# Attention and GELU MLP on one normalised input: one summed channel tile ahead of the logits in three of four chunks, q's weights in five loads, and a new order of pieces

## The chip, the cores and the metric

One core of a Trainium2 chip runs the kernel. The metric is the device time of one execution in microseconds (us). The engines work side by side, each through its own list of instructions in order: TensorE (PE, matmuls; PEld is its weight load), VectorE (DVE), ScalarE (ACT), GpSimd (POOL) and SyncE (SP, which here only issues DMAs).

## The reference

The input is normalised once; attention over a dilated window and an MLP both read it, and both are added to the input.

```python
def _A_ref(x, wqkv, wo):                      # x: (1, 2048, 640)
    H = 32; Dh = D // H                       # Dh = 20
    W, dil = 8, 2
    q, k, v = ...                             # x @ wqkv, each (B, H, S, Dh)
    idx = pos[:, None] - off[None, :]         # off = 0, 2, .. 14
    mask = idx >= 0
    kg, vg = ...                              # k and v at idx
    logits = jnp.einsum("bhsd,bhswd->bhsw", q, kg) * scale
    logits = jnp.where(mask[None, None, :, :], logits, -1e9)
    attn = _softmax(logits, axis=-1)
    o = jnp.einsum("bhsw,bhswd->bhsd", attn, vg)
    return (...)(o) @ wo
def _B_ref(x, w1, b1, w2, b2):                # 640 -> 1536 -> 640
    return _gelu(x @ w1 + b1) @ w2 + b2
xn = _layernorm(x, axis=-1)
return x + _A_ref(xn, A_wqkv, A_wo) + _B_ref(xn, B_w1, B_b1, B_w2, B_b2)
```

## The kernel before

The 2048 positions are worked in four chunks of 512, each of four blocks `j` of 128. Channels lie on partitions in five tiles of 128, permuted so that each partition belongs to one of 32 heads: the sum over a head's 20 channels is the sum over five tiles and then over four partitions.

Every step is a small function, recorded as a named piece, and `ORDER` (L40 to L72) lists the pieces by hand. Each engine gets its instructions in that order; between engines only semaphores hold. The names, with n the chunk: `st`, `su`, `sq`, `rs`, `rc`, `xn` are the normalisation (block statistics on DVE, L209, or on ACT, L221 and L228, for block 1 of chunk 0 and for chunks 2 and 3; square root on ACT, reciprocal on DVE). `tp` and `tc` transpose the result to `xnT`, for chunk 0 on PE with copies by DVE and ACT (L280, L285), later by DMA on SP (L292). `wa`, `wb` are matmuls on constants at the start.

- q, k, v: chunk 0 in blocks and pairs of blocks (`ga`, `gb`, `gd`, `ge`, copies `gc`, L349; `hj`, copies `hc`, L380); later chunks by `pj` and the copies `pc` on ACT (L336, L400). Their PSUM banks come from a pool of four, `psA`, shared with the MLP's `f1` (L586), which ACT empties with the GELU `ge` (L602).
- logits: `qk{n}{j}{h}` on DVE multiplies q with k shifted to four of the eight window places (128x2560, into `half`, L433). `pa{n}{j}{k}` on DVE adds channel tiles in place (L465): k = 0 adds tiles 2 and 3 to 0 and 1, k = 1 adds tile 1 to 0, and k = 2, which no chunk uses before, adds tile 4 to 0. How many tiles are left is `KEPT`. `lg` sums what is left over the four partitions of each head with the matrix `head_of`: for each tile kept, two halves h and four blocks j, eight matmuls of 128x512, block j writing 32 of the rows of `L` (L474). `cl` copies `L` out on ACT.
- softmax: `m`, `mx`, `ex` (ACT), `ss`, `ri`, `at`. Then `xd{n}{j}` on SP broadcasts block j's weights to all partitions by DMA (L548), into `ax` or, for odd chunks, into spent room of `x_sb`.
- values: `av{n}{j}{h}` on DVE (L557, again into `half`), `aa` adds the two halves (an accumulating DMA on POOL, L567, for chunks 0 to 2, DVE in chunk 3), `ab` and `ot` on DVE (L573, L577) make `oT`.
- output: `o{n}{bl}{pc}` on PE: pc 0 to 3 are the MLP's second product, pc 4 is `oT` times wo (L622 for 512 columns, L624 for 128). `oc` copies out on ACT, and `od` adds it to the output by an accumulating DMA on POOL (L635); the input and b2 get there by `xp` (SP) and `xb` (POOL).

`half` has one buffer for all chunks: a chunk's `av` may write a block only when the chunk's `lg` has read it, and the next chunk's `qk` only when `ot` has read it.

At the start SP issues block 0 of x, then q's weights as one load, k's, blocks 2 and 3, v's, chunk 1 of x and w1; ACT issues block 1 and b1.

Of the kernel before, what the change touches and what calls it, by code (L numbers as in the profile page):

```python
# [20 lines left out]
KT, FT = D // P, F // P  # L21
# [16 lines left out]
COLS = ((0, 2), (2, 4), (4, 5))  # L38

ORDER = """  # L40
wa ho st00a sum1 st00 rs00 rc00 neg1 sq1 xn00a tp00a wb xn00b tp00b mean1 tc00a rs01 rc01 tb b1 tc00b ga gb2 xn01 tp01
tc01a tc01b gb3 gb4 gd ge gc4 gc1 hj100 st02a st02 rs02 hc100 st03a st03 hj101 gc0 rc02 xn02 rs03 hj102 rc03 xn03
hc101 hc102 tp02 tc02 hj202 tp03 tc03 hj201 hc201 hj010 st11a hc010 st13a hc202 st12a hj012 hc012 hj112 hc112 f10_3
st11 ldx hj011 f10_9 st10a st10 st12 st13 rs1 qk011 ge0_3 rc1 xn13 pad01 qk000 qk001 tc13 ge0_9 xn12 tc12 pa000 qk010
pk hj110 hc110 hj111 hc111 hc011 qk030 qk031 qk021 pad11 xn11 f10_10 tc11 pa010 xn10 qk020 tc10 ge0_10 f10_2 ge0_2
hj200 hc200 f10_0 pa030 f10_6 f10_11 su20 ge0_6 xp2 su22 su23 pj111 pc111 ge0_0 su21 ng2 pj110 pc110 pj104 pc104 sq23
pj120 pc120 ge0_11 sq20 pj114 pc114 pj113 pc113 pa001 pa020 pa021 pj102 pc102 pa031 pa011 lg0 cl0 mask m0 hj212 hc212
pj123 pc123 mx0 ex0 pj103 pc103 pj112 pc112 ss0 ri0 pj101 pc101 pj100 pc100 qk110 qk100 ld2 ldo xb2 sq22 qk130 pj124
pc124 hj211 sq21 qk121 rs2 pj121 pc121 hj210 hc210 rc2 f10_8 qk131 hc211 f11_9 ge1_9 xp0 xn20 f10_1 ge0_1 f10_7 tc20
f11_5 xb0 qk120 xn21 tc21 qk101 ge1_5 ge0_7 xn23 tc23 ge0_8 xn22 qk111 o000 f11_8 ge1_8 pa130 at0 pa110 f11_0 ge1_0  # L50
pa100 pad12 f10_5 ge0_5 f11_3 ge1_3 f11_6 su32 tc22 pa120 pa101 xd00 f10_4 su33 pj214 pc214 pa111 su31 su30 pj210
pc210 pad21 xd02 ge0_4 pj211 pa121 ge1_6 pa131 lg1 pj200 pad02 av000 av001 aa00 pc200 ng3 sq32 sq31 sq30 av020 pc211
av021 xd01 av011 o001 pj213 pc213 pj122 pj202 pc202 av010 o002 ab00 ot00 pj204 pj212 o003 pc212 pj223 pj222 cl1 aa02
xd03 pc122 av030 av031 m1 mx1 sq33 rs3 pj201 rc3 pc204 o004 oc00 ab02 ot02 pj224 ex1 o020 aa01 aa03 ss1 ri1 xn33 at1
ab01 ot01 ab03 o021 o022 o023 o024 xp1 tc33 pc201 xn32 tc32 pc222 oc02 ot03 od02 f12_7 xd10 av101 pad22 xd12 pc223
f11_4 xn30 o030 o031 o032 o033 pc224 xd11 xn31 pj221 av100 aa10 o034 oc03 f11_2 o010 ge1_4 tc31 av120 o011 o012 o013
o014 av110 av111 aa11 ge2_7 pc221 od03 f11_7 ge1_7 pj203 pc203 ge1_2 xd13 f11_1 av131 tc30 pj311 pc311 av130 aa13
pj304 f12_3 ge2_3 pj310 pc310 pc304 ge1_1 pj302 av121 aa12 ab10 ot10 f11_10 pc302 ge1_10 pj313 pc313 qk201 qk200 pj312
pj314 ab11 ot11 qk210 pc312 oc01 od01 f13_8 ge3_8 qk211 o130 ab13 pa200 pc314 f11_11 ge1_11 qk231 f12_6 o131 ot13
qk230 xb3 f12_0 ge2_0 pj220 pc220 o132 o133 o134 oc13 pj301 pc301 pa210 ge2_6 ab12 ot12 qk221 pj300 pj324 pc300 qk220  # L60
f13_7 xb1 pc324 od13 pa211 pj303 o120 pa230 pa220 pa231 pc303 pad31 pa221 pa201 lg2 ge3_7 cl2 qk301 f12_2 m2 mx2 ex2
f13_10 f12_8 ge2_8 o121 o122 o123 od00 o124 oc12 qk310 ss2 pj320 pc320 qk311 ri2 at2 xd22 xd20 o110 o111 qk331 o112
o113 o114 oc11 od11 qk330 f13_6 ge3_6 f12_5 ge2_5 ge3_10 o100 ge2_2 qk320 pa330 qk321 pa320 f13_5 f12_4 ge3_5 pj322
f13_2 o101 ge2_4 qk300 xd21 pc322 pa321 o102 o103 o104 ge3_2 pa300 pa301 pa331 pa310 pa311 lg3 f13_3 av210 f13_9 oc10
od10 od12 av211 aa21 ge3_3 f12_10 ge2_10 xd23 av230 av200 f12_1 ge2_1 ge3_9 av231 aa23 f12_9 ge2_9 f13_1 ge3_1 f13_4
f12_11 av201 av221 ab21 ge3_4 av220 pj321 o210 o211 o212 f13_0 ot21 ge2_11 o213 o214 f13_11 cl3 m3 mx3 ex3 pad32 ss3
ri3 at3 xd32 oc21 o200 o201 pc321 o202 aa20 ab20 ot20 ab23 ot23 ge3_0 aa22 o203 o310 o204 oc20 pj323 pc323 ab22 ot22
av320 o230 o231 o232 o233 o234 od20 oc23 av321 aa32 xd30 o311 o312 od21 ab32 o220 o221 o222 o223 o224 ge3_11 xd31
av311 od23 o313 av301 av310 oc22 od22 o320 o321 o322 o323 av300 ot32 o324 oc32 aa31 ab31 ot31 o314 oc31 o300 o301 o302
xd33 od32 aa30 o330 o303 ab30 ot30 o304 av331 av330 aa33 ab33 o331 o332 o333 ot33 od31 xl o334 oclo oc30 ohi ochi ochd  # L70
od30
""".split()  # L72


# [1 line left out]
def kernel(  # L76
# [55 lines left out]
    def load_w(s):  # L132
        nc.sync.dma_start(wqkv[s][:], wqkv_v[:, :, s * D : (s + 1) * D])
# [43 lines left out]
    mask = consts.tile([H, W, MW], BF16, name="mask")  # L177
# [610 lines left out]
```

## Time and profile before

| | |
|---|---|
| median of three runs | 207.1 us (206.86 to 207.37) |
| the profiled execution | 207.49 us, span of its trace 205.7 us |
| PE busy | 200.8 us, 1285 matmuls |
| DVE busy | 175.4 us |
| ACT busy | 127.7 us |
| first 128x512 product of chunk 0's DVE logits (L433) | starts at 17.40 us |
| q's weights (800 KB, one DMA) | 5.5 us from issue to landing |

A group's row in the profile reads: line, engine, operation, out<-in, shapes, count, then total busy us and mean ns of one, then the engine's idle time just before these instructions and what ended it. A row of waits reads: who waited, for whom, us in total, times, longest. A row of the chain reads: start, length, what.

### The profile page before, as it was taken

What the parts mean: (1) busy time and instruction counts of PE and PEld (TensorE: products, weight loads), DVE (VectorE), ACT (ScalarE), POOL (GpSimd) and SP (SyncE); (2) the same over time, 40 slices, a digit from 0 to 9 for tenths busy, and PEclk for the clock granted to TensorE, in tenths of its full rate; (3) what the DMA queues carried; (4) which work ended last, traced back from release to release, by engine and by line L of the source; (5) the groups of instructions that cost most, each with busy time, mean ns of one, the idle gap of its engine ahead of it and who ended that gap; (6) DMA issues with size and microseconds to landing.
All of it is one profiled execution on the core that took longest, in us unless ns stands there. A gap on an engine that the chain in (4) does not pass through costs nothing.

```text
span 205.7 us, 3262 instructions
## 1 busy us (share of the span) xinstructions
PE 200.8 (98%) x1285; PEld 112.2 (55%) x1285; DVE 175.4 (85%) x214; ACT 127.7 (62%) x242; POOL 34.4 (17%) x49
## 2 busy tenths in 40 slices
PE   7899999999999999999999999999999999999994
PEld 2797745565445555555555554555444555555552
DVE  3489999379998989949999994999979979799981
ACT  5488999899999879916466344834616854221210
POOL 2000000050000422102703303001023420311210
DMA  6999389969258599899996965018209998931244
GB/s 210 390 397 370 75 232 326 403 102 185 64 116 264 99 186 181 142 192 124 207 198 113 144 107 64 0 16 182 41 0 132 162 193 162 192 41 17 30 52 64
DMA packets 27335, 31.77 MB, mean 154 GB/s; under 512 B 9272, under 2 KB 22072, under 8 KB 27320
## 3 DMA queue, kind: packets, MB, share of 16 engines
q0 software_dynamic: 7408, 12.78, 39.4%
q1 hardware_dynamic: 19600, 18.58, 31.4%
q8 instruction: 10, 0.16, 0.3%
q10 hardware_dynamic: 312, 0.20, 0.3%
q14 instruction: 5, 0.04, 0.1%
HBM read 10.00 MB, written 7.54 MB: 85 GB/s over the span
## 4 chain that ended last, share of the span: by engine, by line
PE 95%; DMA 3%; SPq 0%; DVE 0%; issue 0%
PE lo L622 29%; PE hps L586 25%; PE pps L336 24%; PE hi L624 7%; PE gps L380 7%; DMA wq_sb<-in_A_wqkv_dram 3%; PE L L474 2%; PE gps L349 1%; PE tp L280 0%; SPq L130 0%; DVE osb L652 0%
## 5 line engine op out<-in xcount | busy, mean ns | idle before, releaser
L586 PE MATMUL hps<-xnT,w_sb 128*128 128x512 bf16 x240 | 55.6, 379 | 0.0
L433 DVE TENSOR_TENSOR half<-qT,kT 128x2560 bf16<-128x2560 bf16 x32 | 46.2, 1482 | 2.9 <-PE L L474 2.8
L622 PE MATMUL lo<-w_sb,hT 128*128 128x512 bf16 x144 | 41.3, 379 | 0.0
L586 PEld LDWEIGHTS <-w_sb 128*128 128x128 bf16 x240 | 22.9, 98 | 26.3 <-issue 0.8
L629 ACT CAST osb<-lo 128x512 bf16<-128x512 f32 x15 | 8.8, 587 | 36.8 <-PE hi L624 18.5
L624 PE MATMUL hi<-w_sb,hT 128*128 128x128 bf16 x144 | 31.5, 219 | 0.0
L602 ACT ACTIVATE hT<-hps,b1T 128x512 bf16<-128x512 f32 x36 | 24.0, 683 | 10.7 <-PE hps L586 10.7
L465 DVE TENSOR_TENSOR half<-half 128x2048 bf16<-128x2048 bf16 (+1 forms) x32 | 29.0, 952 | 0.2
L635 POOL DMA_DIRECT2D out_dram<-osb x15 | 13.6, 973 | 77.1 <-ACT osb L630 68.5
L557 DVE TENSOR_TENSOR half<-vT,x_sb 128x2560 bf16<-128x2560 bf16 x16 | 22.8, 1485 | 4.4 <-DMA x_sb<-e 3.0
L557 DVE TENSOR_TENSOR half<-vT,ax 128x2560 bf16<-128x2560 bf16 x16 | 22.8, 1485 | 2.3 <-PE L L474 1.4
L622 PEld LDWEIGHTS <-hT 128*128 128x128 bf16 x144 | 14.1, 98 | 16.8
L622 PE MATMUL lo<-wo,oT 128*128 128x512 bf16 x80 | 23.1, 379 | 0.0
L567 POOL DMA_DIRECT2D half<-half x12 | 14.3, 1195 | 48.9 <-DVE half L557 48.5
L336 PE MATMUL pps<-xnT,wv_sb 128*128 128x512 bf16 x75 | 18.5, 379 | 0.0
L336 PE MATMUL pps<-xnT,wq_sb 128*128 128x512 bf16 x75 | 18.3, 379 | 0.0
L336 PE MATMUL pps<-xnT,wk_sb 128*128 128x512 bf16 x75 | 17.7, 379 | 0.0
L624 PE MATMUL hi<-wo,oT 128*128 128x128 bf16 x80 | 16.9, 219 | 0.0
L173 ACT ACT_TABLE_LOAD x12 | 15.4, 1283 | 0.9 <-PEq L772 0.7
L624 PEld LDWEIGHTS <-hT 128*128 128x128 bf16 x144 | 14.1, 98 | 2.2
L573 DVE TENSOR_TENSOR half<-half 128x1280 bf16<-128x1280 bf16 x16 | 13.1, 820 | 1.3 <-DMA half<-half 1.2
L622 PEld LDWEIGHTS <-oT 128*128 128x128 bf16 x80 | 7.8, 98 | 9.4
(91 smaller groups left out, 263.7 us busy)
## 6 DMA issues: line engine op xcount, KB each, us to landing
half<-half POOLq DMA_DIRECT2D x12, 640.0 KB, 7.1
w_sb<-in_B_w_dram SPq DMA_DIRECT2D x4, 960.0 KB, 11.0
out_dram<-osb POOLq DMA_DIRECT2D x15, 160.0 KB, 4.0
ax<-e SPq DMA_DIRECT2D x8, 256.0 KB, 4.8
x_sb<-e SPq DMA_DIRECT2D x8, 256.0 KB, 4.8
out_dram<-b2bc POOLq DMA_DIRECT2D x3, 640.0 KB, 8.7
x_sb<-in_A_x_dram SPq DMA_DIRECT2D x1, 1280.0 KB, 12.9
out_dram<-x_sb SPq DMA_DIRECT2D x2, 640.0 KB, 8.7
```

Of the source, the lines that this page charges most:

```text
L173: nc.scalar.activation(warm[:], nc.const_aps.tensor(0.0, [P, 1], F32), func)
L336: nc.tensor.matmul(ps[:], lhsT=wqkv_p[which][:, ti, to, :], rhs=xnT[:, ti, :], start=(ti == 0), stop=(ti == KT - 1),)
L380: nc.tensor.matmul(ps[:, to - a, :], lhsT=wqkv_p[which][:, ti, to, :], rhs=tiles["xnT", 0][:, ti, pair * 2 * P : (pair + 1) * 2 * P], star ...
L433: nc.vector.tensor_tensor(out=half[:, j, h], in0=q[:, :, at].unsqueeze(1).to_broadcast([P, W // 2, KT, P]), in1=window(k, h, at), op=ALU.mult,
L465: nc.vector.tensor_tensor(out=kept, in0=kept, in1=gone, op=ALU.add)
L557: nc.vector.tensor_tensor(out=half[:, j, h], in0=window(qkv_tile(n, 2), h, cs), in1=ax_view(n)[:, j, ws, :].unsqueeze(2).to_broadcast([P, ...
L567: nc.gpsimd.dma_start(a, b, accum_op=ALU.add, max_dma_last_dim=CUT)
L586: nc.tensor.matmul(ps[:], lhsT=w1_sb[:, ti, ft * P : (ft + 1) * P], rhs=tiles["xnT", n][:, ti, :], start=(ti == 0), stop=(ti == KT - 1),)
L602: nc.scalar.activation(hT, tiles["hps", n, ft][:], ACT.Gelu_apprx_tanh, bias=b1T[:, ft : ft + 1], scale=1.0)
L622: nc.tensor.matmul(lo[:], lhsT=lhs, rhs=rhs[:, 0:CH], start=first, stop=last)
L624: nc.tensor.matmul(hi[:, 0 : D - CH], lhsT=lhs, rhs=rhs[:, CH:D], start=first, stop=last)
L635: nc.gpsimd.dma_start(rows, tiles["osb", n, bl][:], accum_op=ALU.add)
```

## The change

- `KEPT`: chunks 1 to 3 keep one channel tile instead of two. Each of their blocks gets a third sum, `pa{n}{j}2` (tile 4 added to tile 0, 128x1024), twelve in all, and each of their `lg` has eight matmuls instead of sixteen. Chunk 0 is as before.
- q's weights come by five DMAs, one for each 128 rows of the weights, instead of one.
- `ORDER` is a new list. Apart from the twelve new sums it holds the same pieces.

```diff
-KEPT = (2, 2, 2, 2)
+KEPT = (2, 1, 1, 1)
...
-    load_w(0)
+    for a in range(5):
+        ks = slice(a * KT // 5, (a + 1) * KT // 5)
+        nc.sync.dma_start(wqkv[0][:, ks, :], wqkv_v[:, ks, 0:D])
     load_w(1)
```

The new order, where the text speaks of it (the start; around chunk 0's logits; chunk 1's; the softmax and values of chunk 1; chunk 2's and chunk 3's logits):

```diff
-wa ho st00a sum1 st00 rs00 rc00 neg1 sq1 xn00a tp00a wb xn00b tp00b mean1 tc00a rs01 rc01 tb b1 tc00b ga gb2 xn01 tp01
-tc01a tc01b gb3 gb4 gd ge gc4 gc1 hj100 st02a st02 rs02 hc100 st03a st03 hj101 gc0 rc02 xn02 rs03 hj102 rc03 xn03
-hc101 hc102 tp02 tc02 hj202 tp03 tc03 hj201 hc201 hj010 st11a hc010 st13a hc202 st12a hj012 hc012 hj112 hc112 f10_3
+wb sum1 neg1 wa st00a st00 rs00 rc00 sq1 rs01 xn00a tp00a tb xn00b tp00b tc00b tc00a ho ga gb2 mean1 rc01 xn01 b1 tp01
+tc01b tc01a st02a st02 gb3 gb4 gc0 gd ge gc1 rs02 st03a st03 ldx hj102 hc102 hj101 pad01 gc4 rs03 rc03 xn03 hc101
+hj100 hc100 tp03 tc03 hj202 rc02 xn02 tp02 tc02 hj201 hc201 hj012 hc012 hc202 st10a hj112 hc112 hj110 hc110 st10 st13a
...
-hj200 hc200 f10_0 pa030 f10_6 f10_11 su20 ge0_6 xp2 su22 su23 pj111 pc111 ge0_0 su21 ng2 pj110 pc110 pj104 pc104 sq23
+f10_11 ge0_11 qk031 su22 hj200 hc200 f10_10 f10_6 ge0_6 su23 su20 ng2 pa021 ge0_10 pj103 pc103 pj120 sq21 pc120 pj113
...
+f11_0 xn21 tc21 f11_6 ge1_6 xn23 f11_9 pa131 ge0_5 pa121 f10_4 ge0_4 su33 ge1_9 o000 o001 o002 tc23 pj212 pa101 pa111
+pa102 su30 su31 su32 pj211 pc211 pa112 pj214 pc214 pa122 pa132 lg1 xd00 av000 ng3 sq30 av001 av021 aa00 pj213 pc213
...
+ab00 ot00 av031 pj222 aa03 pj201 pc201 pj224 sq31 rs3 rc3 cl1 m1 pj200 pc200 f11_11 o003 o004 oc00 mx1 pj203 ex1 o020
+o021 o022 o023 od00 ab02 ot02 o024 xn32 tc32 pc222 ss1 ri1 at1 xd10 pc224 xn30 oc02 xn33 f11_10 pj220 pc220 ab03 ot03
+o030 pc203 o031 o032 o033 o034 ab01 ot01 tc30 av100 av101 aa10 xn31 xd12 f12_0 av120 oc03 xd11 av110 av111 o010 aa11
+ge1_10 f12_8 ge2_8 xd13 av121 av130 av131 o011 o012 pad22 ab10 aa13 tc33 aa12 f11_1 ge1_1 pad21 qk201 pj221 pc221
...
+pj301 pa211 pj303 pa230 pc303 pc304 pa220 o132 o133 o134 pa212 pa221 pc322 xb1 pa231 pc301 pa222 f13_7 oc13 od13 pa232
+lg2 cl2 qk300 od02 qk320 qk311 f13_10 ge3_10 o120 o121 o122 o123 m2 mx2 o124 oc12 qk310 od12 qk330 f12_6 o110 ge3_7
...
+ge3_2 pa301 pc320 pa322 f12_11 f13_6 ge3_6 pa302 pa332 pa312 lg3 ge2_11 cl3 f12_9 xd21 av210 f13_0 f12_1 ge2_1 f12_10
```

More of the change, by code (lines that the diff above doesn't have):

```diff
@@ L40 @@
 ORDER = """
-wa ho st00a sum1 st00 rs00 rc00 neg1 sq1 xn00a tp00a wb xn00b tp00b mean1 tc00a rs01 rc01 tb b1 tc00b ga gb2 xn01 tp01
-tc01a tc01b gb3 gb4 gd ge gc4 gc1 hj100 st02a st02 rs02 hc100 st03a st03 hj101 gc0 rc02 xn02 rs03 hj102 rc03 xn03
-hc101 hc102 tp02 tc02 hj202 tp03 tc03 hj201 hc201 hj010 st11a hc010 st13a hc202 st12a hj012 hc012 hj112 hc112 f10_3
-st11 ldx hj011 f10_9 st10a st10 st12 st13 rs1 qk011 ge0_3 rc1 xn13 pad01 qk000 qk001 tc13 ge0_9 xn12 tc12 pa000 qk010
-pk hj110 hc110 hj111 hc111 hc011 qk030 qk031 qk021 pad11 xn11 f10_10 tc11 pa010 xn10 qk020 tc10 ge0_10 f10_2 ge0_2
@@ L46 @@
-hj200 hc200 f10_0 pa030 f10_6 f10_11 su20 ge0_6 xp2 su22 su23 pj111 pc111 ge0_0 su21 ng2 pj110 pc110 pj104 pc104 sq23
[L47 to L70, printed above, removed]
@@ L71 @@
-od30
+wb sum1 neg1 wa st00a st00 rs00 rc00 sq1 rs01 xn00a tp00a tb xn00b tp00b tc00b tc00a ho ga gb2 mean1 rc01 xn01 b1 tp01
+tc01b tc01a st02a st02 gb3 gb4 gc0 gd ge gc1 rs02 st03a st03 ldx hj102 hc102 hj101 pad01 gc4 rs03 rc03 xn03 hc101
+hj100 hc100 tp03 tc03 hj202 rc02 xn02 tp02 tc02 hj201 hc201 hj012 hc012 hc202 st10a hj112 hc112 hj110 hc110 st10 st13a
+st13 f10_3 st12a st12 st11a st11 rs1 f10_0 ge0_0 qk000 rc1 xn13 pk tc13 xn12 tc12 qk001 qk010 hj010 hc010 pa000 hj011
+qk011 ge0_3 hj111 hc111 hc011 qk020 qk030 xp0 f10_9 ge0_9 qk021 pa010 xn10 tc10 pa020 f10_2 pa001 ge0_2 xn11 tc11 su21
@@ new lines @@
+f10_11 ge0_11 qk031 su22 hj200 hc200 f10_10 f10_6 ge0_6 su23 su20 ng2 pa021 ge0_10 pj103 pc103 pj120 sq21 pc120 pj113
+pj110 ldo ld2 xb0 sq23 xp2 xb2 pj104 pc104 pa030 pa011 pc113 pj102 pc102 pc110 pa031 lg0 cl0 pj112 pc112 mask m0 mx0
+ex0 ss0 ri0 at0 xd01 xd02 pj123 pc123 pad11 pj100 pc100 pj101 pj114 pc114 pc101 pj111 pc111 qk130 qk131 sq20 qk101
+sq22 pj124 pc124 pa130 qk110 hj210 hc210 f11_8 pad02 rs2 rc2 pj121 pc121 hj211 hc211 hj212 qk111 qk100 f11_3 qk121
+hc212 f11_5 qk120 f10_1 ge1_8 xn22 tc22 ge0_1 pa100 ge1_3 f10_5 xn20 tc20 pa120 f10_8 ge1_5 pa110 ge0_8 f10_7 ge0_7
@@ new lines @@
+f11_0 xn21 tc21 f11_6 ge1_6 xn23 f11_9 pa131 ge0_5 pa121 f10_4 ge0_4 su33 ge1_9 o000 o001 o002 tc23 pj212 pa101 pa111
+pa102 su30 su31 su32 pj211 pc211 pa112 pj214 pc214 pa122 pa132 lg1 xd00 av000 ng3 sq30 av001 av021 aa00 pj213 pc213
+pj210 pc212 pc210 pj204 pc204 pad12 sq33 pj202 pc202 av020 aa02 pj122 xp1 pc122 ge1_0 xd03 sq32 av011 av030 av010 aa01
+ab00 ot00 av031 pj222 aa03 pj201 pc201 pj224 sq31 rs3 rc3 cl1 m1 pj200 pc200 f11_11 o003 o004 oc00 mx1 pj203 ex1 o020
+o021 o022 o023 od00 ab02 ot02 o024 xn32 tc32 pc222 ss1 ri1 at1 xd10 pc224 xn30 oc02 xn33 f11_10 pj220 pc220 ab03 ot03
@@ new lines @@
+o030 pc203 o031 o032 o033 o034 ab01 ot01 tc30 av100 av101 aa10 xn31 xd12 f12_0 av120 oc03 xd11 av110 av111 o010 aa11
+ge1_10 f12_8 ge2_8 xd13 av121 av130 av131 o011 o012 pad22 ab10 aa13 tc33 aa12 f11_1 ge1_1 pad21 qk201 pj221 pc221
+ge2_0 o013 f11_2 ge1_2 o014 f11_7 pad31 ge1_7 f12_7 ge2_7 tc31 pj310 ot10 qk200 ab11 qk211 pj314 pc314 pj311 pc311
+pj313 ge1_11 pc313 pj300 pc300 ot11 pj223 pc223 pa200 pj302 pc302 pj312 pc312 od03 qk210 qk231 f11_4 ge1_4 pj324 pc324
+oc01 ab13 pa210 ot13 ab12 pj304 qk221 qk230 ot12 f12_3 ge2_3 pc310 pa201 pj322 o130 o131 qk220 f13_8 ge3_8 pa202 od01
@@ new lines @@
+pj301 pa211 pj303 pa230 pc303 pc304 pa220 o132 o133 o134 pa212 pa221 pc322 xb1 pa231 pc301 pa222 f13_7 oc13 od13 pa232
+lg2 cl2 qk300 od02 qk320 qk311 f13_10 ge3_10 o120 o121 o122 o123 m2 mx2 o124 oc12 qk310 od12 qk330 f12_6 o110 ge3_7
+ex2 qk321 ss2 pa320 ri2 qk301 f12_4 at2 xd22 ge2_6 xd23 o111 pad32 f13_3 qk331 o112 o113 o114 oc11 pj320 pa330 ge3_3
+f12_5 pa321 f13_5 ge3_5 pa300 o100 ge2_5 o101 o102 ge2_4 pa310 o103 o104 oc10 od10 f12_2 pa331 f13_2 xb3 ge2_2 pa311
+ge3_2 pa301 pc320 pa322 f12_11 f13_6 ge3_6 pa302 pa332 pa312 lg3 ge2_11 cl3 f12_9 xd21 av210 f13_0 f12_1 ge2_1 f12_10
@@ new lines @@
+ge2_10 f13_4 od11 ge3_4 ge2_9 f13_1 ge3_1 av211 aa21 pj321 pc321 av230 ge3_0 av231 aa23 o210 o211 o212 o213 xd20 av201
+av200 aa20 o310 o311 m3 ab21 mx3 ex3 ot21 o214 oc21 od21 av221 f13_9 ge3_9 ss3 ri3 at3 av220 ab20 ot20 ab23 ot23 o200
+o201 o202 pj323 pc323 o203 aa22 o204 oc20 xd31 av311 av310 aa31 ab31 o312 o230 o231 o232 o233 xd33 av330 xd32 o234
+oc23 o330 o331 av321 o220 o221 o222 od23 ab22 ot22 o223 o224 oc22 f13_11 ge3_11 o320 od20 o321 o313 av320 aa32 ab32
+o322 o323 od22 ot32 o324 oc32 ot31 o314 oc31 o300 o301 od32 od31 xd30 av300 av301 aa30 o302 ab30 ot30 o303 o304 o332
@@ L72 @@
+oc30 av331 aa33 ab33 ot33 o333 xl o334 oclo ohi ochi ochd od30
 """.split()
```

## The prediction

> **What bounds the kernel now.** I read the page's busy shares and its chain first, then who waited on TensorE (PE) and on VectorE (DVE), then the chain in order of time at the stages that the change touches.
>
> ```profile
> PE 200.8 (98%) x1285; PEld 112.2 (55%) x1285; DVE 175.4 (85%) x214; ACT 127.7 (62%) x242; POOL 34.4 (17%) x49
> PE 95%; DMA 3%; SPq 0%; DVE 0%; issue 0%
> ...
> PE tp L280 <- DVE xn L265: 0.8, 1, 0.8
> PE idle L446 <- PEq L772: 0.8, 1, 0.8
> PE gps L349 <- DMA wq_sb<-in_A_wqkv_dram: 0.6, 1, 0.6
> ```
>
> The last three rows are all the waits of PE, and all lie before 6.76 us. From there to 203 us PE runs without a gap, so a matmul removed comes off the end at its full price, and a wait of PE goes onto the end at its full price. The other engines cost something only where they make PE wait.
>
> ```profile
> 1.20 5.51 DMA wq_sb<-in_A_wqkv_dram
> 6.76 1.03 PE gps L349 x15
> ...
> 10.02 2.73 PE gps L380 x25
> 12.75 0.28 PE tp L280 x5
> ...
> 36.60 0.98 PE L L474 x16
> ```
>
> The chain (start, length): q's whole weight load ends the start-up; 50 q and 25 k matmuls follow; the logits of a chunk cost 0.98 us of PE.
>
> ```profile
> L474 PE MATMUL L<-half,head_of 128*32 128x512 bf16 x64 | 4.3, 381 | 0.0
> L465 DVE TENSOR_TENSOR half<-half 128x2048 bf16<-128x2048 bf16 x16 | 19.3, 1219 | 0.1
> L465 DVE TENSOR_TENSOR half<-half 128x1024 bf16<-128x1024 bf16 x16 | 10.3, 684 | 0.1
> ```
>
> Groups with shapes apart: sixteen logit matmuls of 381 ns take 0.98 us together, so they don't run one after another: the four blocks `j` write four groups of 32 rows beside each other. The 1024-wide sum is the operation that the change adds.
>
> ```profile
> 90.58 2.89 DVE L557 TENSOR_TENSOR half<-vT,x_sb 128x2560 bf16<-128x2560 bf16 x2 [3.01 <-DMA x_sb<-e]
> 128.12 1.49 DVE L433 TENSOR_TENSOR half<-qT,kT 128x2560 bf16<-128x2560 bf16 x1 [2.83 <-PE L L474]
> 152.77 9.90 DVE L557 TENSOR_TENSOR half<-vT,ax 128x2560 bf16<-128x2560 bf16 x7 [1.40 <-PE L L474]
> ```
>
> Where DVE idles (brackets: idle time and what ended it). Ahead of chunk 2's logits DVE was done at 128.12 - 2.83 = 125.29 while PE came to them at 126.98: 1.7 us to spare. Ahead of chunk 3's: done at 151.37, PE at 151.97: 0.6 us.
>
> **Logits, chunks 1 to 3 (removes).** Eight matmuls instead of sixteen, two groups of four fewer. A 128x512 matmul of L336 or L586 advances the chain by 1.08/5 = 0.216 us, so two groups are 0.43 us; half of 0.98 is 0.49. I take 0.45, times 3: **-1.35 us**, all on the path.
>
> **Sums on DVE (adds).** 3 x 4 `pa..2`, each 684 ns less the 0.08 us by which neighbours overlap (two of 1485 ns take 2.89): 12 x 0.60 = 7.2 us, 2.4 per chunk. DVE idles some 16 us in waits from 17 us on. What hides the sums must be seen at each logit stage, since PE reaches `lg` by its own order:
> - lg1: today DVE's last sum of chunk 1 ends at 63.91 and PE starts at 63.92: nothing to spare. The new order puts `o001` and `o002` ahead of lg1 (six lo+hi pairs of 0.27: PE comes 1.63 us later) and takes `pj111`, `pj114` from ahead of lg0 for `pj103` (lg0 comes 1.08 us earlier, which shortens DVE's waits around chunk 0's softmax, 2.57 and 1.77 us today, by some 1.3). So +1.63 + 1.3 - 2.4, less 0.1 for the earlier start: 0.4 us to spare.
> - lg2: PE at 126.98 + 0.27 (`pj322` in, `o120` out) - 0.45 - 0.2 (start, lg0's side) = 126.6. DVE works without a break from `av100`: 16 products x 1.40, 12 sums (4 x 1.14, 8 x 0.60), 4 `ab` x 0.74, 4 `ot` x 0.41 = 36.4 us (today's 34.7 + 2.4 gives 37.1). `av100` waits for the broadcast `xd10`. Ahead of it DVE gains four sums (2.4) and sheds `ab01 ot01 ab03 ot03` (2.3), so its issue stays at today's 85.35 or up to 0.6 later. It landed 5.2 us later today, while an output accumulate issued at the same time (85.36) took 6.1; the first broadcasts of chunks 0, 2 and 3 took 3.5 to 3.7. The new order issues that output (`od00`) before `ab02`, ahead of `at1`, several us before `xd10`, so I take 3.7: start at 89.4, sums done at 125.8 to 126.5, **0 to 0.8 us to spare**. With 5.2 they end at 127.3 to 128.0: PE waits 0.7 to 1.4.
> - lg3: `f12_11` and `f13_3` come ahead of it (+2.16), two cheaper logit stages lie behind (-0.9): PE at 153.0. DVE restarts about 0.8 us earlier, when lg2 releases `half`, and needs 2.4 more: 151.37 + 1.6 = 153.0. Even, with up to 0.6 us to spare.
>
> I cost the sums at **0.1 us** (lg0 comes early by 1.08 but its sums hardly do); if the cover fails, the price is the wait at one stage, not 7.2 us.
>
> **q's weights by five DMAs, and the start order.** PE need no longer wait for 0.8 MB: the first 160 KB block landed 2.5 us after issue, so by the same time the pieces land from about 3.9 to at most 6.7. Then `xnT` ends the wait. In the new order ACT does `neg1` (0.19) ahead of `rs00`, so the first `xn` and its copy come 0.1 later than 6.05: PE starts q at 6.2, **-0.55 us**. Given back right after: `tc01b` (ACT) now stands before `tc01a` (DVE), and two copies into one tile go one after the other:
>
> ```profile
> 8.11 0.29 DVE L285 COPY xnT<-tp 128x256 bf16<-128x256 bf16 x1 [1.25 <-PE tp L280]
> 8.43 0.48 ACT L285 COPY xnT<-tp 128x384 bf16<-128x384 bf16 x1 [1.85 <-DVE xnT L285]
> 9.60 0.89 DVE L209 BATCH_NORM_STATS2 stats<-x_sb 128x6 f32<-128x320 bf16 x2 [1.20 <-DMA x_sb<-in_A_x_dram]
> ```
>
> `gd` needs the short one, which now ends 0.48 + 0.29 + steps = 0.9 us after the transposes, with ten matmuls (0.56) to cover: **+0.45**. Then PE is at the next transpose at 12.5 instead of 12.75, but both blocks' statistics, `rs03`, `rc03` and `xn03` need 3.05 us from the landing at 9.6 (last line above): 12.65, **+0.15**. In the built program the loads of SP and ACT share eight landing semaphores in turn, and a load waits until the one eight before it has landed, so k's load now waits for block 0 (0.74 + 2.5 = 3.25, before: issued at 1.67), and blocks 2 and 3 for q's first piece. Behind them stand v, x and w1. I cost that at nothing: the DMA engines are full with q's bytes till at least 5.6, and k is needed at 9.7. If that cover is gone, block 2 lands some 0.5 later and PE waits as much.
>
> The Trainium skill, "DMA: Bandwidth & Descriptors" (Anatomy of one DMA; Rules for kernel authors), gives each DMA a fixed 2.0 us and tells to coalesce small ones, which speaks against five. Its formula gives 2.4 us for 160 KB, near the 2.5 here.
>
> **Other moves** have one answer: equal work in another order. One place looks tight: `pj103` waits for the PSUM bank that `hc200` empties, behind `su21`, `ge0_11` and `su22` on ACT (0.74, 0.68, 0.74 plus the accumulator reads): **+0.2** (0 to 0.4).
>
> **Sum:** -1.35 - 0.55 + 0.45 + 0.15 + 0.1 + 0.2 = -1.0 us. The profiled execution took 207.49 us (span 205.7 and 1.8 around it) and should become 206.5; the median of before is 207.1, so 206.1.
>
> **Rivals.**
> 1. *PE waits for the sums at one logit stage*, likeliest lg2, with `xd10` landing as late as today: +0.7 to 1.4, **207.1**. For: no stage has over 0.8 us to spare. Against: the accumulate that shared the DMA engines moves away. Chance 0.25.
> 2. *Slower: DVE's chain of DMAs becomes the bound.* Each chunk's DVE chain holds four accumulates `half<-half` (median 7.1 us to landing) and four broadcasts. With 2.4 us less slack per chunk, accumulates of 7.5 us and broadcasts of 5.5 us leave the sums late at lg2 (1.2) and `oT` late for the `o..4` matmuls behind (1.0): 206.1 + 2.2 = **208.3**. It decides from broadcasts at 5.2 with accumulates above 7. Against: waits on `half<-half` cost DVE only 1.2 us in all today. Chance 0.12.
> 3. *The logits don't get cheaper*, because entering and leaving the 32-column shape makes up the 0.98 us: 206.1 + 1.35 = **207.5**. Against: four groups at 0.216 already explain 0.86. Chance 0.03.
> 4. *Five DMAs pay their fixed time one after another*: five times 2.5 us from 1.2 is 13.7 against 6.7, **213**. Against: k, block 2 and v land 2.0, 0.8 and 2.1 us apart today though each takes over 7 from its issue, so latencies overlap. Chance 0.02. This is what the Trainium skill's rule on that page would mean if it held for queued loads too; today's landings speak against it.
>
> **How the numbers follow.** Forecast 206.1, chance 0.58. About 0.3% (0.6 us) is what can be told from no change. The forecast's case lies below 206.5 (faster); rivals 1 and 3 are within 0.3%; 2 and 4 slower: 0.58, 0.28, 0.14. Low end: half of the give-backs fail to come, 205.6. High end: rival 1 whole with its upper price, 207.5; rival 2 and 4 stay outside.
>
> **What would show it.** Chain: three logit stages of 0.53 us, chunk 0's still 0.98. First q matmul near 6.2 with no wait on `wq_sb`; a PE wait on DVE's `xnT` of 0.45 near 8.3. DVE busy 182.6 us. Waits of PE on `half` at L474 would show rival 1. The forecast is wrong if PE waits over 0.6 us more than the places listed.

## The result, and the profile after

The changed kernel takes 209.65 us (median of six runs) where the kernel before takes 207.26 in the same comparison: 1.0114 times as long, 95% interval 1.0072 to 1.0157. One of the six runs, at 213.18, was in a slow state and is not in the ratio. The changed kernel is slower; the range of the prediction ended at 207.5. The profiled execution of the changed kernel took 209.43 us, its span is 207.7.

The page's shares and chain of the changed kernel, and then its rows of who waited on PE:

```profile
PE 200.3 (96%) x1239; PEld 112.0 (54%) x1261; DVE 182.1 (88%) x226; ACT 128.6 (62%) x242; POOL 34.5 (17%) x49
PE 85%; ACT 6%; DMA 3%; DVE 1%; SPq 1%; issue 1%
```

```profile
PE tp L282 <- DVE xn L267: 1.1, 1, 1.1
PE idle L448 <- PEq L774: 0.8, 1, 0.8
PE gps L382 <- DMA wk_sb<-in_A_wqkv_dram: 0.3, 1, 0.3
PE pps L338 <- ACT vT L397: 0.3, 1, 0.3
```

Lines are numbered two higher than before. DVE's busy time is as forecast (182.6 was expected), and no row names `half`: the twelve added sums are hidden, but for 0.16 us at chunk 2's logits (below). New are a wait of 1.1 us for the normalised block 2, a wait for k's weights and one for the PSUM bank of `pj103`. The chain in order of time (start, length, what):

```profile
4.04 7.25 DMA x_sb<-in_A_x_dram
11.31 0.90 DVE stats L211 x2
...
14.50 0.45 PE tp L282 x5
...
37.87 0.98 PE L L476 x16
...
67.89 0.55 PE L L476 x8
...
129.14 0.71 PE L L476 x8
...
155.68 0.55 PE L L476 x8
```

The start-up is no longer ended by q's weights but by the load of blocks 2 and 3, issued at 4.04 and landed at 11.29; in the trace of before it was issued at 2.23 and landed at 9.58. Block 2 is transposed at 14.50 instead of 12.75. The three cheaper logit stages are there (0.55, 0.71 and 0.55). In the kernel before they were:

```profile
63.92 1.07 PE L L474 x16
...
127.06 0.98 PE L L474 x16
...
151.97 0.98 PE L L474 x16
```

So the gain came and was overpaid, most of it in the first 15 us.

The timeline of SP's queue in the changed kernel, and under it the windows of one microsecond at the start (window, busy PE, PEld, DVE, ACT, POOL with counts, granted clock, share of the DMA engines that was busy, GB/s):

```profile
1.21 2.31 SPq L141 DMA_DIRECT2D wq_sb<-in_A_wqkv_dram  x5
3.56 0.43 SPq L133 DMA_DIRECT2D wk_sb<-in_A_wqkv_dram  x1
4.04 0.52 SPq L130 DMA_DIRECT2D x_sb<-in_A_x_dram  x1
5.65 0.37 SPq L133 DMA_DIRECT2D wv_sb<-in_A_wqkv_dram  x1
```

```profile
3.00:4.00 1.00, 1.00 (x4) 0.31 (x3) 0.78 (x2) 0.41 (x1) 0.00 (x0) 1.00 1.00 344
4.00:5.00 1.00, 1.00 (x4) 0.29 (x2) 0.45 (x3) 0.97 (x5) 0.00 (x0) 1.00 0.69 128
5.00:6.00 1.00, 1.00 (x10) 0.80 (x8) 0.67 (x3) 0.94 (x3) 0.00 (x0) 1.00 0.91 319
```

In the kernel before, the same three windows moved 328, 386 and 374 GB/s. Its row of the second:

```profile
4.00:5.00 1.00, 0.65 (x6) 0.32 (x4) 0.54 (x3) 0.93 (x5) 0.00 (x0) 1.00 1.04 386
```

In the changed kernel the DMA engines are a third idle from 4 to 5 us and move 128 GB/s. From 2 to 10 us they moved 2.53 MB instead of 2.93; at 390 GB/s the difference is 1.03 us of the 1.7 by which blocks 2 and 3 land later. The rest lies in whose bytes moved. Up to that landing the engines moved 2.81 MB before (293 GB/s over 9.58 us) and 3.06 MB here (271 over 11.29). So 0.25 MB more of other loads went ahead of it, which is 0.65 us at the same rate; why they did no view shows.

The last rows of the two timelines that end the program, before and changed:

```profile
203.31 0.37 ACTq L657 DMA_DIRECT2D out_dram<-osb  x1
```

```profile
204.43 0.37 ACTq L659 DMA_DIRECT2D out_dram<-osb  x1
```

The last output is issued 1.12 us later, but the span is 1.94 longer (205.73 and 207.67): from that issue to the end the program takes 3.24 instead of 2.42. That is a second loss of 0.82 us, which the prediction had not looked at.

### The profile page after: what moved, and what is told of

Read it like the earlier page. It is cut to its first block, busy times and chain, and to the rows that moved or that the text cites. A ratio compares the mean times of both kernels' runs of the same rounds, so it can differ in the third digit from the quotient of the medians.

```text
span 207.7 us, 3212 instructions
## 1 busy us (share of the span) xinstructions
PE 200.3 (96%) x1239; PEld 112.0 (54%) x1261; DVE 182.1 (88%) x226; ACT 128.6 (62%) x242; POOL 34.5 (17%) x49
## 4 chain that ended last, share of the span: by engine, by line
PE 85%; ACT 6%; DMA 3%; DVE 1%; SPq 1%; issue 1%
PE lo L624 27%; PE pps L338 23%; PE hps L588 21%; PE hi L626 8%; DMA x_sb<-in_A_x_dram 3%; PE gps L382 3%; ACT hT L604 2%; ACT xn L265 1%; PE L L476 1%; SPq L141 1%; DVE stats L211 1%; ACT trash L223 1%; ACT L175 1%; ACT kT L397 1%; ACT qT L397 0%
## 5 line engine op out<-in xcount | busy, mean ns | idle before, releaser
L624 PE MATMUL lo<-w_sb,hT 128*128 128x512 bf16 x140 | 40.5, 379 | 0.0
L467 DVE TENSOR_TENSOR half<-half 128x1024 bf16<-128x1024 bf16 (+1 forms) x44 | 35.9, 876 | 0.0
L637 POOL DMA_DIRECT2D out_dram<-osb x15 | 15.1, 1052 | 68.2 <-ACT osb L632 68.1
L624 PE MATMUL lo<-wo,oT 128*128 128x512 bf16 x75 | 22.2, 379 | 0.0
L307 POOL DMA_DIRECT2D out_dram<-b2bc x4 | 6.0, 1495 | 46.6 <-DMA b2bc<-in_B_b_dram 34.9
```

Of the source, the lines that this page charges most:

```text
L467: nc.vector.tensor_tensor(out=kept, in0=kept, in1=gone, op=ALU.add)
L624: nc.tensor.matmul(lo[:], lhsT=lhs, rhs=rhs[:, 0:CH], start=first, stop=last)
L637: nc.gpsimd.dma_start(rows, tiles["osb", n, bl][:], accum_op=ALU.add)
```

## The experiments

Times are medians; ratios are to the kernel before, run beside it (207.22 to 207.26). A ratio is not the quotient of the two medians (for two loads that would be 1.0040, and the ratio is 1.0016); where the two differ, the interval counts. Positions are those of one traced execution of each kernel.

| kernel | us | ratio, 95% interval | blocks 2 and 3 issued, landed | chunk 0's `lg` starts |
|---|---|---|---|---|
| changed | 209.65 | 1.0114 (1.0072 to 1.0157) | 4.04, 11.29 | 37.87 |
| new order, one load | 207.08 | 0.9996 (0.998 to 1.0011) | 2.24, 9.54 | 36.18 |
| old order, five loads | 210.22 | 1.0138 (1.0109 to 1.0168) | 4.04, 11.99 | 38.80 |
| changed, two tiles kept | 211.12 | 1.0185 (1.0156 to 1.0213) | 4.07, 11.80 | 38.37 |
| old order, one tile kept | 215.10 | 1.0380 (1.0364 to 1.0395) | 2.23, 9.01 | 36.13 |
| old order, four tiny loads | 208.39 | 1.0073 (1.0048 to 1.0098) | 5.96, 9.06 | 36.84 |
| old order, four loads by partition | 210.66 | 1.0166 (1.0148 to 1.0184) | 3.60, 10.49 | 38.77 |
| new order, two loads | 208.06 | 1.0016 (0.9982 to 1.0051) | 2.71, 10.88 | 37.28 |
| hybrid order, one load | 206.44 | 0.9960 (0.9945 to 0.9976) | 2.24, 9.04 | 35.32 |
| hybrid, one filler later | 207.12 | 0.9993 (0.9964 to 1.0023) | 2.23, 8.95 | 35.57 |
| changed, five loads on two queues | 209.49 | 1.0104 (1.0064 to 1.0143) | 4.26, 10.85 | 37.44 |
| old order, k by five loads | 208.71 | 1.0057 (1.0035 to 1.0080) | 6.11, 9.07 | 36.95 |

### Which part costs: one load, old order, two tiles, one tile

The new order and the sums with q's weights in one load again:

```diff
-    for a in range(5):
-        ks = slice(a * KT // 5, (a + 1) * KT // 5)
-        nc.sync.dma_start(wqkv[0][:, ks, :], wqkv_v[:, ks, 0:D])
+    load_w(0)
```

> The changed kernel with q's weights in one load again, nothing else undone. Theory A (the five loads are the whole loss: k's load and blocks 2 and 3 of x are issued 1.8 us later and land 1.7 us later, PE waits for them): about 2.5 us come back, 206.6 to 207.0, and the first transpose of block 3 is back near 12.7. Theory B (the loss sits in the new order, in copies and sums that PE waits for before 38 us): at least 208.5 as now, with the 2.4 us between the two kernels at chunk 0's logits unchanged.

It takes 207.08, the same as before. So the five loads cost 2.6 us, and the order with the sums gains nothing that can be told. The rows of PE's waits in its trace say where part of the 1.4 us of the logits went:

```profile
PE gps L349 <- DVE xnT L285: 0.3, 1, 0.3
PE gps L349 <- DVE rstd L251: 0.3, 1, 0.3
```

The first, at 8.80, is the forecast wait for `tc01a` behind `tc01b`. The second ends at 6.60, right after q's one load has landed (6.55): the row names DVE, but by the times it is the wait for q that before had too. Chunk 0's `lg` stands 0.66 later than before, net of the 1.08 us of work moved past it, and the end of the program is 0.36 longer (both below).

The other way round, the kernel before with q's weights by five loads:

```diff
-    load_w(0)
+    for a in range(5):
+        ks = slice(a * KT // 5, (a + 1) * KT // 5)
+        nc.sync.dma_start(wqkv[0][:, ks, :], wqkv_v[:, ks, 0:D])
```

> The kernel before with the five loads alone, old order and two channel tiles. Theory A: slower than before by 1.3 to 2, so 208.5 to 209.3. Theory B: 207.3 or a little less (PE need not wait for the whole of q's weights: 206.8).

It takes 210.22, more than either theory had: alone, the five loads cost 3.0 us. Its first q matmul starts at 6.37, earlier than the 6.76 of before, but PE then waits for k and for block 2:

```profile
PE gps L382 <- DMA wk_sb<-in_A_wqkv_dram: 1.6, 1, 1.6
PE tp L282 <- DVE xn L267: 0.6, 1, 0.6
```

The changed kernel without the third sums:

```diff
-KEPT = (2, 1, 1, 1)
+KEPT = (2, 2, 2, 2)
...
-pa102 su30 su31 su32 pj211 pc211 pa112 pj214 pc214 pa122 pa132 lg1 xd00 av000 ng3 sq30 av001 av021 aa00 pj213 pc213
+su30 su31 su32 pj211 pc211 pj214 pc214 lg1 xd00 av000 ng3 sq30 av001 av021 aa00 pj213 pc213
...
```

> The changed kernel without the twelve new sums and with sixteen logit matmuls in every chunk, order and five loads kept. If one tile saves 0.45 us of PE per chunk and DVE's sums are wholly hidden: 1.3 us slower than the changed kernel, 211.0. If the sums cost as much as the matmuls save: the same, 209.7. If the sums are part of the loss: faster than the changed kernel.

It takes 211.12, 1.5 us more than the changed kernel. All its logit stages are back at 0.98, and in this execution blocks 2 and 3 landed 0.5 later as well: 1.13 and 0.5 make the 1.63 us by which its last matmul ends later. The saving is real, and the sums cost next to nothing in the new order.

In the old order they do. The kernel before with the third sum put right behind the second:

```diff
-KEPT = (2, 2, 2, 2)
+KEPT = (2, 1, 1, 1)
...
-pa100 pad12 f10_5 ge0_5 f11_3 ge1_3 f11_6 su32 tc22 pa120 pa101 xd00 f10_4 su33 pj214 pc214 pa111 su31 su30 pj210
+pa100 pad12 f10_5 ge0_5 f11_3 ge1_3 f11_6 su32 tc22 pa120 pa101 pa102 xd00 f10_4 su33 pj214 pc214 pa111 pa112 su31 su30 pj210
...
```

> The kernel before with one channel tile in chunks 1 to 3 and each new sum right behind the sum before it, old order, one load. By the slack read from the trace of before (none at chunk 1's logits, 1.7 us at chunk 2's, 0.6 at chunk 3's) PE waits some 2.4, 0.3 and 1.5 us there and the kernel is slower by 2 to 4 us: 209.5 to 211. If DVE's sums are hidden in any order: 205.9.

It takes 215.10, 4 us more than was expected: PE waits for the sums four times, and after the waits the granted clock falls, which the expectation had left out. The rows of PE's wait and of the windows around chunk 1's logits (the number before the DMA share is the granted clock):

```profile
PE L L474 <- DVE half L465: 4.4, 4, 2.0
```

```profile
64.00:66.00 2.00, 0.49 (x2) 0.09 (x1) 1.93 (x4) 1.45 (x4) 0.00 (x0) 1.00 0.98 339
66.00:68.00 2.00, 1.61 (x8) 0.56 (x8) 2.00 (x3) 0.00 (x0) 0.00 (x0) 0.78 0.18 67
68.00:70.00 2.00, 2.00 (x8) 0.83 (x7) 2.00 (x2) 0.80 (x3) 0.56 (x1) 0.50 0.00 0
70.00:72.00 2.00, 2.00 (x11) 1.07 (x10) 2.00 (x3) 1.94 (x5) 0.63 (x1) 0.87 0.44 81
```

PE works 0.49 of the two microseconds from 64, and then the granted clock is 0.78, 0.50 and 0.87. Behind the longest wait, 2.0 us ahead of chunk 3's logits, it is 0.57 from 159 to 161 us and 0.58 from 161 to 163; behind the wait of 0.5 us at chunk 2's it stays at 1.00. The waits are 4.4 us, the kernel lost 7.8. So it is the new order that hides the third sum, and the order could not be left out of the change. Other places for the sum in the old order were not tried.

### Why five loads of the same bytes are slower

Two theories: the loads behind q's are issued later (each issue takes SP 0.47 us), or pieces of 128 rows are slow in themselves. The first alone, with q in one load and four loads of 3 KB behind it:

```diff
     load_w(0)
+    spare = consts.tile([MW, 4, P], BF16, name="spare")
+    for a in range(4):
+        nc.sync.dma_start(spare[0:FT, a, :], B_b1.rearrange("(t p) -> t p", p=P))
```

> The kernel of before with q's weights in one load, and behind that load, ahead of k's, four more loads of 3 KB each (the channel bias again, into a tile that nothing reads), so that k's load and blocks 2 and 3's load are issued four places (about 1.9 us) later, as in the changed kernel, while q's bytes come in one piece. Theory 'late issue' (what costs is that k's and blocks 2 and 3's loads are issued 1.8 us later; each issue takes 0.46 us on SP's queue): k's issue at 3.5, blocks 2 and 3's at 4.0, the latter landing at 11.0 to 11.8 instead of 9.6, the transposes of block 2 waiting, total 208.5 to 210. Theory 'slow pieces' (what costs is that q's bytes come in pieces of 128 rows of 1280 bytes each, some of whose packets take 0.4 to 1.2 us): the engines stay full with q's one load until about 5.5, blocks 2 and 3 land at 9.6 to 10.1, total 207.1 to 207.6.

Timeline rows of this kernel:

```profile
3.41 0.41 SPq L133 DMA_DIRECT2D wk_sb<-in_A_wqkv_dram  x1
5.96 0.39 SPq L130 DMA_DIRECT2D x_sb<-in_A_x_dram  x1
...
9.08 0.89 DVE L212 BATCH_NORM_STATS2 stats<-x_sb 128x6 f32<-128x320 bf16 x2 [0.94 <-DMA x_sb<-in_A_x_dram]
```

Blocks 2 and 3 are issued at 5.96, 3.7 us later than before, and their statistics start at 9.08: earlier than the 9.60 of before, and earlier than both theories had it. The late issue does not delay the landing, since q's one load keeps the engines at 343 to 392 GB/s from 3 to 6 us. "Late issue" by itself is wrong. The kernel is still 1.2 us slower (its span 1.04), of which PE accounts for 0.24 (its last matmul); 0.8 comes after it, at the end of the program (below).

Then the second theory, with the same five pieces, but of k and behind q's one load:

```diff
     load_w(0)
-    load_w(1)
+    for a in range(5):
+        ks = slice(a * KT // 5, (a + 1) * KT // 5)
+        nc.sync.dma_start(wqkv[1][:, ks, :], wqkv_v[:, ks, D : 2 * D])
```

> The kernel of before with q's weights in one load and k's in five by k-tile, so that the same number of pieces of the same size stands behind q's 820 KB instead of ahead of them; blocks 2 and 3's load is issued four places later, as in the changed kernel. Four loads more also turn the ring of landing semaphores by four places, which cost 0.87 us at the end of the program in the kernel with four tiny loads. Theory 'thin feed': q's bytes keep the engines full (390 GB/s from 4 us on) while k's pieces are issued, blocks 2 and 3 land at 9.5 to 10.2, the transposes of block 2 wait no more than 0.5 longer, total 208.1 to 208.6. Theory 'slow pieces': under 330 GB/s while k's pieces move, blocks 2 and 3 land at 10.7 or later, total 209 to 210.5.

```profile
4.00:5.00 1.00, 1.00 (x4) 0.30 (x2) 0.50 (x4) 0.94 (x5) 0.00 (x0) 1.00 1.05 389
5.00:6.00 1.00, 1.00 (x11) 1.00 (x10) 0.72 (x4) 0.97 (x3) 0.00 (x0) 1.00 1.07 391
6.00:7.00 1.00, 1.00 (x17) 0.88 (x16) 0.78 (x4) 0.53 (x2) 0.00 (x0) 1.00 1.07 389
7.00:8.00 1.00, 1.00 (x22) 1.00 (x20) 0.29 (x1) 0.02 (x1) 0.00 (x0) 1.00 0.98 301
```

The engines move 389 to 391 GB/s until 7 us. Up to 6.09 us these are mostly still q's bytes; the five pieces then land between 6.49 and 8.17, 0.42 us apart, and 164 KB in 0.42 us is 390 GB/s. "Slow pieces" is wrong too. The rate falls only at 7 us, when the bytes already issued run out: blocks 2 and 3's load had to wait until 6.11 for its landing semaphore (eight are taken in turn). They still landed at 9.07. Of its 1.2 us of span over the kernel before, 0.4 is PE's and 0.8 the end of the program's. So while a large load stands in front, the later issue and the size of the pieces cost PE 0.2 to 0.4 us in these two kernels, and not the 1.85 that splitting q costs (table below). What costs is that the load at the head of the queue is split. That nothing is in reserve then ("thin feed" in the expectations) is a reading of the rates; the next two kernels bear it out only in part.

The pieces issued faster, by two engines:

```diff
-        nc.sync.dma_start(wqkv[0][:, ks, :], wqkv_v[:, ks, 0:D])
+        (nc.scalar if a % 2 else nc.sync).dma_start(wqkv[0][:, ks, :], wqkv_v[:, ks, 0:D])
```

(with the bias's load moved behind them on ACT)

> The changed kernel with its five loads of q issued on two engines' queues: pieces 0, 2 and 4 on SP's, 1 and 3 on ACT's, ahead of the bias's. The pieces are the same, and all of q is issued by 2.7 instead of 3.5 us, k's load at 2.6 instead of 3.56, blocks 2 and 3's at 3.1 instead of 4.04. Theory 'thin feed' (pieces of 164 KB issued 0.47 us apart give the DMA engines no more than 350 GB/s and nothing in reserve, so they run empty between 4 and 5 us, at 128 GB/s): the rate from 4 to 5 us rises above 280 GB/s, blocks 2 and 3 land at 9.8 to 10.4, total 208.2 to 208.9. Theory 'slow pieces' (a load of 128 rows is slow whenever it is issued): rate and landing stay at 128 to 200 GB/s and 11 to 11.5, total 209.3 to 210.

```profile
4.00:5.00 1.00, 1.00 (x9) 0.54 (x7) 0.96 (x3) 0.75 (x3) 0.00 (x0) 1.00 1.02 356
5.00:6.00 1.00, 0.09 (x2) 0.00 (x0) 0.30 (x2) 0.97 (x5) 0.00 (x0) 1.00 0.96 235
6.00:7.00 1.00, 0.57 (x6) 0.45 (x7) 0.88 (x4) 0.90 (x3) 0.00 (x0) 1.00 0.95 320
```

All of q is issued by 2.6 us and the hole from 4 to 5 is gone (356 GB/s, as "thin feed" had it). It reappears at 5 to 6, because k's load, meant for 2.6, was issued at 3.83: its semaphore was that of the first piece, which landed at 3.81. Blocks 2 and 3 land at 10.85, between the two forecasts. The median, 209.49, is not better. In this kernel blocks 0 and 1 land 0.8 and 1.0 later too (3.99 and 4.53), and PE waits 1.3 us for block 0 at 6.43. The nine runs lie between 207.9 and 211.0, so its times decide little; its rates speak for thin feed.

Two loads in place of five:

```diff
-    for a in range(5):
-        ks = slice(a * KT // 5, (a + 1) * KT // 5)
+    for ks in (slice(0, 2), slice(2, KT)):
```

> The changed kernel with q's weights in two loads (k-tiles 0 and 1, then 2 to 4) in place of five: one more issue on SP's queue than with one load. With one load the new order took 207.1, with five 209.65. Theory 'late issue': blocks 2 and 3's load is issued 0.46 us later than with one load and lands at 10.0, total 207.5 to 207.8. Theory 'slow pieces': the cost comes with the first split, whatever the number of pieces: blocks 2 and 3's load lands near 11, total 208.3 to 209.3.

The median is 208.06, between the two forecasts, and by the interval it can't be told from before. Blocks 2 and 3 land at 10.88, as "slow pieces" had it. PE also waits for q's second load, which was issued whole at 2.14 and lands only at 8.02, where q's one load landed at 6.71 before:

```profile
PE gps L350 <- DMA wq_sb<-in_A_wqkv_dram: 1.3, 1, 1.3
```

The rate from 4 to 5 us is 276 GB/s with 0.82 of the engines busy, although all of q was issued by 2.14 and k's load by 2.67. Thin feed does not explain this alone. In the changed kernel and in this one, single packets of 1280 bytes, which mostly take 55 ns, took 0.3 to 0.8 us between 3.8 and 5.2 us (twelve of them in the changed kernel, three in this one, none in the trace of before). With k by five loads twelve such packets come from 7.3 to 9.0 us, where its rate falls. Why is open.

A split that keeps all k-tiles in each load, by 32 partitions:

```diff
-    load_w(0)
+    for a in range(4):
+        ps = slice(32 * a, 32 * (a + 1))
+        nc.sync.dma_start(wqkv[0][ps, :, :], wqkv_v[ps, :, 0:D])
```

> The kernel of before with q's weights in four loads of 32 partitions each, every load with all five k-tiles, in place of one load. The later loads on SP's queue are issued three places (1.4 us) later, but the bytes of each piece lie in other rows than those of the five loads by k-tile. Theory 'late issue': k's issue at 3.1, blocks 2 and 3's load lands at 10.7 to 11.3, total 208.3 to 209.6. Theory 'slow pieces of 128 rows': blocks 2 and 3's load lands at 9.6 to 10, total 207.1 to 207.6.

It takes 210.66, more than both theories had, but for a reason of its own, so it does not tell them apart:

```profile
4.00:5.00 1.00, 1.00 (x4) 0.29 (x3) 0.38 (x3) 0.97 (x5) 0.00 (x0) 1.00 1.03 218
5.00:6.00 1.00, 1.00 (x11) 1.00 (x10) 0.63 (x4) 0.92 (x3) 0.00 (x0) 1.00 1.12 238
6.00:7.00 1.00, 0.34 (x5) 0.14 (x2) 0.78 (x4) 0.48 (x1) 0.00 (x0) 1.00 1.08 236
7.00:8.00 1.00, 0.60 (x11) 0.63 (x12) 0.00 (x0) 0.00 (x0) 0.00 (x0) 1.00 1.00 371
```

The engines are busy all the time and move 218 to 238 GB/s; a packet takes 89 to 98 ns (medians by microsecond) until q's last piece has landed at 7.27, and 55 afterwards. The Trainium skill, "SBUF — State Buffer" (Door 1: The DMA port swizzle), says that 32 neighbouring partitions reach half of the ports and gives some 218 GB/s for them; the trace agrees. Also every q matmul needs all partitions, so PE waits 1.1 us for the last piece.

### A start that keeps the gain, and the end of the program

One load, the old order up to `hj201` (block 3's transposes; `ldx` and `pad01` stand just ahead of `hj201`), and then the new order's pieces as far as they are not yet issued:

```diff
-wb sum1 neg1 wa st00a st00 rs00 rc00 sq1 rs01 xn00a tp00a tb xn00b tp00b tc00b tc00a ho ga gb2 mean1 rc01 xn01 b1 tp01
-tc01b tc01a st02a st02 gb3 gb4 gc0 gd ge gc1 rs02 st03a st03 ldx hj102 hc102 hj101 pad01 gc4 rs03 rc03 xn03 hc101
...
+wa ho st00a sum1 st00 rs00 rc00 neg1 sq1 xn00a tp00a wb xn00b tp00b mean1 tc00a rs01 rc01 tb b1 tc00b ga
+gb2 xn01 tp01 tc01a tc01b gb3 gb4 gd ge gc4 gc1 hj100 st02a st02 rs02 hc100 st03a st03 hj101 gc0 rc02 xn02
...
```

> One load for q, the old order of pieces up to and with 'hj201' (the work up to the last of block 3's transposed copies), then the new order's pieces that are not yet issued, with chunks 1 to 3 keeping one tile of logits. The new order as a whole with one load took 207.1, that is it gained 1.3 us at three logit stages and lost it elsewhere. Theory 'the new order loses it in its first 15 us' (two waits for the transposed copies of block 0 of 0.3 us, block 3's transposes ahead of block 2's): the old start gives it back, total 206.2 to 206.7, transposes of block 2 at 12.8 or before, no wait of PE for a DVE piece near 8.3. Theory 'it loses it by the placing of the pieces after 15 us': total 206.9 to 207.4.

It takes 206.44 and is faster than the kernel before (0.9945 to 0.9976 of its time) and than the changed one. Chunk 0's `lg` starts at 35.32, 0.86 earlier than with the new start, and the three stages behind are 0.55 each:

```profile
35.32 1.11 PE L L474 x16
...
65.48 0.55 PE L L474 x8
...
126.73 0.55 PE L L474 x8
...
153.11 0.55 PE L L474 x8
```

About 0.5 us of the 0.86 may be this execution's own: its loads landed 0.5 earlier, as they did in four other profiles of one-load kernels. Still, all its four runs (206.33 to 206.70) lie below all ten of the new order with one load (206.80 to 208.05).

From the last output's issue to the end of the span this kernel takes 2.7 us, the new order with one load 2.8, the kernel before 2.4. The trace's records of the end show why: POOL's drain ends 1.3 us after its last output has landed, and in the new order that output is issued 2.6 us before ACT's last one instead of 3.3. To try this, three matmuls of the last block are put behind `oc30`:

```diff
-o231 o232 o233 xd33 av330 xd32 o234 oc23 o330 o331 av321 o220 o221 o222 od23 ab22 ot22 o223 o224 oc22 f13_11 ge3_11
+o231 o232 o233 xd33 av330 xd32 o234 oc23 o330 av321 o220 o221 o222 od23 ab22 ot22 o223 o224 oc22 f13_11 ge3_11 o320
...
-av301 aa30 o302 ab30 ot30 o303 o304 o332 oc30 av331 aa33 ab33 ot33 o333 xl o334 oclo ohi ochi ochd od30
+aa30 o302 ab30 ot30 o303 o304 o332 oc30 av331 aa33 ab33 o331 ot33 o333 xl o334 oclo ohi ochi ochd od30
```

> The hybrid order with one load for q (206.44), with one piece moved: three matmuls of the last block, 'o331' (0.65 us of PE), stand behind 'oc30' instead of ahead of it, so that block 30's copy and POOL's last output are 0.65 us earlier against the end. What is tested is the end of the program: after the last landing it took 0.88 us in the old order and 1.3 in the new one, where POOL's drain ends 1.3 us after its last output's landing and came last. Theory 'POOL's last output is too late': PE ends 0.1 later (a wait of the block 29 matmuls for their transposed values), the drain ends 0.55 earlier, the end after the last landing takes 0.9 instead of 1.25, total 206.2. Theory 'the end's length is of other origin': it stays 1.25, total 206.5 to 206.6.

```profile
PE lo L622 <- DVE oT L577: 1.1, 1, 1.1
```

The end is back at 2.4 us (issue at 203.44, span 205.8), as the first theory had it. But the three matmuls had covered a wait, which is 1.1 us in this trace and not the 0.1 expected; the kernel gains nothing (207.12). Its ten runs lie between 206.09 and 208.79 and the traced one took 207.64, so the wait may be shorter in others.

The rest of the changed kernel's longer end comes with the number of loads. At the end SP waits for the eight landing semaphores one after another in a fixed order, 0.065 us each. Before, the last two outputs hold the last two of the eight; four loads more turn the ring, and they hold the third and fourth, with four waits still to come after the last landing's. In the kernel with the tiny loads and in the one with k by five, where q is not split at all, the end takes 3.2 us as well. In all these SP also pauses 0.45 us around its drain; what it does there no row shows.

## Why the prediction was wrong

The spans' difference, by differences of positions in the three traces; the first line is net of the 1.08 us of work moved past `lg0`:

| | order and sums (one load, against before) | five loads (changed, against one load) | both |
|---|---|---|---|
| up to chunk 0's logits | +0.66 | +1.69 | +2.35 |
| logit stages of chunks 1 to 3 | -1.38 | +0.16 | -1.22 |
| last matmul's end | -0.73 | +1.85 | +1.12 |
| from there to the span's end | +0.36 | +0.46 | +0.82 |
| span | -0.37 | +2.31 | +1.94 |

(The first two lines make up the third to within 0.01.)

- **The step that failed** is the one on the loads behind q's: "I cost that at nothing: the DMA engines are full with q's bytes till at least 5.6". They were not: 128 GB/s from 4 to 5 us. The issue times came much as the prediction had them (k's at 3.56 for 3.25, blocks 2 and 3's right behind the landing of q's first piece at 4.00); the cover did not. I had taken the cover from the trace of before, where it is made by one load of 800 KB that is issued whole at 1.62. The change removes that load, so it removes the cover. The price that I named for its loss, 0.5 us, was also too small: the load of blocks 2 and 3 landed 1.7 later, because not only its issue moved (which by the tiny loads delays no landing) but 0.4 MB went unmoved and 0.25 MB of other loads went ahead. With q in one load again (same order, same sums) blocks 2 and 3 land at 9.54 and 2.6 us come back, which is what shows the step. Why the engines run dry behind split loads stays partly open.
- **The start's gain**, -0.55, was an accident of one execution. The first q matmul starts at 6.44 here, 0.32 earlier than in the trace of before, and at 6.37 in the old order with five loads. But in seven profiles of kernels with one load it starts between 6.16 and 6.76, with a median of 6.39, and the trace of before is the latest of the seven. There was hardly a wait to remove.
- **Logits**, -1.35: measured -1.38 with one load (chunk 1's stage had taken 1.07 before, not 0.98). The size was right, and rival 3 is out (the kernel with two tiles kept shows it from the other side).
- **Sums**, +0.1: 0.16, all at chunk 2's logits, which take 0.71 instead of 0.55. In that trace DVE's last sum ends at 129.20, 0.13 us after PE had begun the stage. It is the stage that the prediction called likeliest; `xd10` landed after 4.4 us, between the 3.7 taken and the 5.2 feared. Rivals 1 and 2 did not come. Their prices left the clock out: in the old order with one tile kept, a wait of 2.0 us brought it to 0.57 behind it, one of 0.5 us did not move it.
- **The new start's give-backs**, 0.45 + 0.15 + 0.2: 0.66 by `lg0`, with a wait of 0.3 for `tc01a`. In the changed kernel the wait for the `pj103` bank is 0.26.
- **Rival 4** had the right side and the wrong mechanism: the pieces landed at 4.00, 5.63, 6.05, 6.51 and 8.05, not 2.5 us apart (the prediction itself had them landed by 6.7). The Trainium skill's rule to coalesce ("DMA: Bandwidth & Descriptors", Rules for kernel authors) pointed the right way, but not for a fixed time paid five times: five pieces of k behind a large load cost PE 0.4 us. The fixed time that the prediction quotes stands on that page for DMAs that GpSimd issues; q's pieces were issued by SP.
- **Not in the sum at all** was the end of the program, +0.82. I had counted "what lies around the span" as constant and the matmuls' end as the end.

## What to carry to other kernels

A transfer that hides the issue of later ones does so because it is already queued; a change that splits it must be priced as if its cover were gone. In a start like this one, keep one large load at the head of the queue and put the small ones behind it. Take the slack of a wait at the start from several executions, and count the end of the program too: a few more DMAs anywhere can turn the order in which the last landings are awaited.

## What was not expected of the hardware

- Two waits of PE of 0.95 us with 0.38 us of work between them brought the granted clock to 0.78 and 0.50 for the next 4 us (the old order with one tile kept). The Trainium skill, "TensorE: Matmul & The Clock Gate" (Why this matters for your kernels), warns of gaps over some 3 us; here gaps of a third of that were enough, when they came close together, and so was a single one of 2.0 us ahead of chunk 3's logits (0.57 and 0.58 for 4 us).
- The same 128-row pieces moved at 390 GB/s behind a large load and left the engines a third idle when they came first, with single packets of 0.3 to 0.8 us. Which queue or memory holds those packets up was not settled.
- Four loads of 3 KB issued before 3.4 us made the end of the program, 200 us later, 0.8 us longer.
